# Attention and two expert layers on one core: token pairs become the outer loop, decoded weights pass through DRAM, partial outputs stay in SBUF

## The chip, the cores and the metric

The kernel runs on one core of one Trainium2 chip. The metric is the device time of one execution in microseconds (us). A measurement of this kernel tells a change of about 0.2% from no change. The engines that the text speaks of are PE (TensorE: matmuls, with PEld for its weight loads), DVE (VectorE), ACT (ScalarE), POOL (GpSimd) and SP (SyncE, which only issues DMAs here). Each works through its own queue of instructions in order; a DMA is issued by an instruction in the queue of SP or ACT and then runs by itself.

## The reference

The first stage is attention with a block-causal mask for 4 batches, 8 heads, 576 positions, 64 wide; its output, 2304 tokens by 512, is x of two feed-forward layers (512 to 2048 to 512):

```python
def _moe_ref(x, w_in, w_out, alpha):
    h = x @ w_in
    g = np.maximum(h, 0.0) + alpha * np.minimum(h, 0.0)
    return g @ w_out

def _moe2_ref(x, w_in, w_out):
    h = x @ w_in
    g = np.where(h > 0.0, h, np.exp(np.minimum(h, 0.0)) - 1.0)
    return g @ w_out

x = attn_out.transpose(0, 2, 1, 3).reshape(2304, 512)
x = _moe_ref(x, w_in, w_out, alpha)
return _moe2_ref(x, w2_in, w2_out)
```

The weights arrive as 64-bit floats.

## The kernel before, in words

Every operand of a matmul is split into a high and a low part (`act.copy` or a cast makes the high part, `low_part` subtracts it), and a product is three matmul passes, `PASSES`: high by high, high by low, low by high.

**Weights.** `load_word` fetches 128 rows of 512 64-bit words (512 KB) and rebuilds 32-bit floats: two activations on ACT (L135, L136), three operations on DVE (L140, L141, L145), one addition on POOL (L150). `load_in` decodes two such words and makes of them the seven Strassen variants of a pair of blocks of w_in: four sums or differences 256 wide (on POOL, L195 to L198), a cast on ACT, a low part on DVE. `load_out` decodes one word of w_out. Both leave their result in SBUF, where three blocks of work use it. There are 64 words in all.

**Attention** takes the first part of the program, with one quarter of layer 1 (4 of 16 blocks of the hidden width) for the tokens that are ready beside it. `plain_tail` is the rest of this quarter: products of the last two token units (512 and 256 tokens), before and among the first Strassen steps.

**The Strassen part** is the other three quarters of layer 1 (`layer == 0`) and all of layer 2 (`layer == 1`). The 2304 tokens are six chunks of N = 384, taken in pairs p = 0, 1, 2; the hidden width is taken in groups g of four blocks of 128. A block of work (layer, g, p) has two halves, each with seven products of six matmuls 384 wide (`product`, L702) in three PSUM banks, so 14 steps and 84 of these matmuls; the `outputs` of the block before (96 matmuls in layer 1, L795; 72 in layer 2, 512 wide, L797) run in between. `BLOCKS` lists 9 blocks of layer 1 and 12 of layer 2: g is the outer loop, p runs forth and back inside.

- `fetch` and `convert` make the seven variants of x for a pair: sums 768 wide (L657), a cast on ACT (L661) and a low part (L97) on DVE or POOL. They run for each change of (layer, p).
- `hiddens` copies a bank to SBUF after four of the seven products (`keep`, L739, on ACT), adds three of these on POOL (`add`, L744) and joins two more on DVE from a bank (L767, L772). One group of results is gated from its bank, three from SBUF, each 384 wide (`gated`): layer 1 has an activation (L715) and a DVE operation (L718); layer 2 an exponential on ACT (L721) and two DVE operations (L722, L723). Then come the cast (L724) and a low part (L97), half of them on POOL.
- `outputs` loads the partial sum z of each of its pieces from DRAM (`zd`, `yd`), adds the bank to it on DVE (L802) and stores it again.

All of these DMAs are issued by SP. In the Strassen part PE's order is that in which the code emits the work; the order on the other engines is laid by the scheduler.

## Time and profile before

| | |
|---|---|
| time, median of 3 runs (lowest to highest) | 1133.84 us (1132.81 to 1134.96) |
| the profiled execution's own time | 1132.23 us |
| its span, first to last instruction | 1130.4 us |
| PE busy, share of the span | 983.5 us, 87% |
| DVE busy | 891.9 us, 79% |
| POOL busy | 694.9 us, 61% |
| ACT busy | 585.4 us, 52% |
| bytes moved by DMA | 170.17 MB, mean 151 GB/s |

The span is 1.8 us shorter than the time of the same execution. Shares are averages over the attention part and the Strassen part, which have different limits, so the stretches have to be read apart. PE's clock is granted by a throttle, at 1.00 (2.4 GHz) or less.

### The profile page before, as it was taken

Reading aid. Unit: us, or ns where it says so; the run is one execution under the profiler, and the core shown is the slowest. Engines: PE = TensorE matmul, PEld = TensorE weight load, DVE = VectorE, ACT = ScalarE, POOL = GpSimd, SP = SyncE. Lnnn points to the kernel's source line nnn. Section 1 sums busy time; section 2 is a strip of 40 time slices with the busy share of each in tenths; the row PEclk is TensorE's granted clock in tenths of the full one; section 3 lists DMA queues with packets and bytes.
Section 4 is the critical chain, followed back from the end, with each engine's and each line's share of the span. In section 5 each row is a group of like instructions: output and inputs, shape, how many; then the busy total and the mean of one; then the engine's idle time right before and its main releaser. Section 6 shows DMA issues by size and latency. Waiting matters only on the chain.

```text
span 1130.4 us, 16131 instructions
## 1 busy us (share of the span) xinstructions
PE 983.5 (87%) x5300; PEld 852.3 (75%) x5300; DVE 891.9 (79%) x1386; ACT 585.4 (52%) x1305; POOL 694.9 (61%) x660
## 2 busy tenths in 40 slices
PE   4878999899984879797988978888988998899998
PEld 3556677567774779797978978877877887798886
DVE  5885576775799989697869798998799879967753
ACT  5875476565455345453545365554645454445431
POOL 5876576672677866457645675585658564835530
PEclk9889999999986899999998989999999999899999
DMA  5453323513775464747473745432354454434333
GB/s 179 146 176 124 95 88 101 192 48 106 241 265 177 163 215 150 236 139 229 152 235 126 222 129 174 131 112 84 117 156 156 140 157 143 137 106 145 107 103 121
DMA packets 101381, 170.17 MB, mean 151 GB/s; under 512 B 15792, under 2 KB 61360, under 8 KB 101296
## 3 DMA queue, kind: packets, MB, share of 16 engines
q1 hardware_dynamic: 101008, 168.87, 47.1%
q8 instruction: 42, 0.69, 0.2%
q14 instruction: 43, 0.35, 0.1%
q10 hardware_dynamic: 288, 0.26, 0.1%
HBM read 121.91 MB, written 47.19 MB: 150 GB/s over the span
## 4 chain that ended last, share of the span: by engine, by line
PE 31%; DVE 30%; DMA 12%; issue 10%; POOL 10%; ACT 5%; SPq 1%; POOLq 0%; ACTq 0%; DVEq 0%
PE bank L702 8%; PE bank L797 7%; DMA wraw<-w 6%; DVE xr L657 4%; PE bank L483 3%; DVE xv L97 3%; PE pair L338 3%; PE bank L601 2%; POOL wword L150 2%; DVE wword L140 2%; DVE g L97 2%; PE bank L612 2%; POOL snap L744 2%; DVE e L722 2%; DVE wword L145 2%
## 5 line engine op out<-in xcount | busy, mean ns | idle before, releaser
L702 PE MATMUL bank<-xv,wv 128*128 128x384 f32 x1764 | 380.6, 354 | 98.6 <-DVE snap L772 54.0
L702 PEld LDWEIGHTS bank<-xv,wv 128*128 128x128 f32 x1764 | 328.8, 199 | 128.5 <-DVE snap L772 64.5
L797 PE MATMUL bank<-wo,g 128*128 128x512 f32 x864 | 228.2, 399 | 2.6 <-ACT g L724 1.9
L744 POOL TENSOR_TENSOR snap<-snap 128x384 f32<-128x384 f32 x126 | 154.5, 1229 | 60.6 <-ACT snap L739 53.5
L797 PEld LDWEIGHTS bank<-wo,g 128*128 128x128 f32 x864 | 163.3, 192 | 28.1 <-ACT g L724 2.4
L795 PE MATMUL bank<-g,wo 128*128 128x384 f32 x864 | 181.0, 350 | 0.5 <-POOL g L97 0.5
L795 PEld LDWEIGHTS bank<-g,wo 128*128 128x128 f32 x864 | 162.0, 199 | 0.8 <-POOL g L97 0.8
L150 POOL TENSOR_TENSOR wword<-wword,wraw 128x512 int32<-128x512 int32 x64 | 95.6, 1495 | 63.7 <-DVE wword L145 47.7
L97 POOL TENSOR_TENSOR g<-e,g 128x384 fp32r<-128x384 f32 x48 | 62.7, 1307 | 95.5 <-ACT g L724 93.8
L104 POOL TENSOR_SCALAR p<-p,stat 128x128 f32<-128x128 f32 (+4 forms) x144 | 84.3, 601 | 49.7 <-DVE stat L397 32.9
L657 DVE TENSOR_TENSOR xr<-xr 128x768 f32<-128x768 f32 x71 | 88.9, 1253 | 27.3 <-POOL xr L657 11.7
L802 DVE TENSOR_TENSOR z<-bank,z 128x384 f32<-128x384 f32 (+1 forms) x126 | 76.3, 605 | 34.1 <-PE bank L797 27.4
L724 ACT CAST g<-e 128x384 fp32r<-128x384 f32 x96 | 48.7, 509 | 97.6 <-DVE e L723 97.6
L739 ACT COPY snap<-bank 128x384 f32<-128x384 f32 x168 | 78.8, 472 | 28.9 <-PE bank L702 27.9
L661 ACT CAST xv<-xr 128x768 fp32r<-128x768 f32 x91 | 75.6, 836 | 29.7 <-DVE xr L657 17.7
L388 ACT ACTIVATE p<-pair,stat 128x128 f32<-128x128 f32 (+4 forms) x144 | 78.1, 555 | 22.6 <-DVE stat L361 22.0
L97 DVE TENSOR_TENSOR xv<-xr,xv 128x768 fp32r<-128x768 f32 x57 | 78.8, 1385 | 13.9 <-ACT xv L661 13.9
L97 POOL TENSOR_TENSOR xv<-xr,xv 128x768 fp32r<-128x768 f32 x34 | 72.3, 2125 | 25.0 <-ACT xv L661 24.8
L97 POOL TENSOR_TENSOR g<-snap,g 128x384 fp32r<-128x384 f32 x36 | 43.7, 1216 | 65.0 <-ACT g L724 65.0
L722 DVE TENSOR_SCALAR e<-e 128x384 f32<-128x384 f32 x96 | 59.3, 620 | 17.6 <-ACT e L721 16.4
L361 DVE TENSOR_REDUCE stat<-pair 128x2 f32<-128x256 f32 (+3 forms) x80 | 63.2, 807 | 5.7 <-PE pair L344 4.1
L145 DVE SCALAR_TENSOR_TENSOR wword<-wraw,wword 128x512 uint32<-128x512 uint32 x64 | 66.3, 1039 | 1.2
(99 smaller groups left out, 1661.5 us busy)
## 6 DMA issues: line engine op xcount, KB each, us to landing
wraw<-w SPq DMA_DIRECT2D x64, 512.0 KB, 4.3
zd<-z SPq DMA_DIRECT2D x84, 192.0 KB, 2.6
xv<-xd SPq DMA_DIRECT2D x42, 384.0 KB, 5.1
z<-zd SPq DMA_DIRECT2D x72, 192.0 KB, 2.6
xr<-zd SPq DMA_DIRECT2D x36, 384.0 KB, 3.3
yd<-z SPq DMA_DIRECT2D x54, 256.0 KB, 2.0
z<-yd SPq DMA_DIRECT2D x54, 256.0 KB, 2.6
xr<-xd SPq DMA_DIRECT2D x28, 384.0 KB, 3.7
```

What stands on the lines that cost most here:

```text
L97: return {"v": dve, "p": pool_e}[eng].tensor_tensor(out=out, in0=x, in1=f32(high), op=ALU.subtract)
L104: return pool_e.tensor_scalar(out, x, 1.0 if scale is None else scale, 1.0, ALU.mult, ALU.mult)
L145: dve.scalar_tensor_tensor(out=wi, in0=high, scalar=0xC0000000, in1=wi, op0=ALU.bitwise_and, op1=ALU.bitwise_or)
L150: pool_e.tensor_tensor(out=w, in0=w, in1=units, op=ALU.add)
L388: act.activation(out=out, in_=x, func=AF.Exp, bias=stat[:, k:k + 1], accum_out=stat[:, SUMS + 2 * k:SUMS + 2 * k + 1])
L657: tt = lambda eng, out, a, b, op: eng.tensor_tensor(out=out, in0=a, in1=b, op=op)
L702: pe.matmul(bank_, w[:, wp_, IN.index(wname), kc * P:kc * P + P], x[:, xp_, kc, :], start=start and kc == 0 and t == 0, stop=stop and kc = ...
L722: dve.tensor_scalar(g, g, 1.0, -1.0, ALU.min, ALU.add)
L739: act.copy(s, x)
L744: pool_e.tensor_tensor(out=out, in0=x, in1=y, op=ALU.add)
L795: pe.matmul(acc, w_out(0, f, wp_, m * P, P), gs[f, h][:, gp_, :], start=s, stop=e)
L797: pe.matmul(acc, gs[f, h][:, gp_, m * P:m * P + P], w_out(1, f, wp_, 0, DM), start=s, stop=e)
```

## The change

- `BLOCKS`: the pair p is now the outer loop, g the inner one. x's variants are made once for each (layer, p): 6 times; the order before made them 16 times.
- z of a pair stays in SBUF (`zall`) over all its groups; it is stored once per layer and pair, and in layer 1 loaded once per pair.
- A decoded weight goes from a staging tile (one `wvs`, one `wos`) to DRAM (`wvd`, `wod`), and each half-block fetches its variants of w_in (1792 KB), each block its two parts of w_out (1024 KB each), from there. These fetches, those of x and those of z are issued by ACT; raw words and stores are issued by SP, whose order is now that of the code too. The sums of `load_in` move from POOL to DVE, and more words are decoded during attention (four `load_in` and four `load_out`; before two `load_in`).
- `hiddens` has another order of products: two banks accumulate on; three copies (two to c2, one to p1) and three joins on DVE from a bank (L763) replace four copies, three POOL additions and two DVE joins.
- `gated` works on two blocks at once, 768 wide: c2 as a whole, of c1 one half from SBUF and one from the bank. In layer 2 a second activation on ACT takes the place of DVE's L722. All its low parts are DVE's.

```diff
+    def load_out(layer, f):
+        t = stage_p.tile([P, 2, DM], F32R, tag="wo", name="wos")
...
+            def store():
+                j, i = divmod(f, 2)
+                if (layer, j) not in wod:
+                    wod[layer, j] = dram.tile([P, 2, 2, DM], F32, name=f"wod{layer}_{j}")
+                nc.sync.dma_start(out=wod[layer, j][:, i], in_=f32(t))
...
-            tt = pool_e.tensor_tensor
+            tt = SUMS_ON.tensor_tensor
...
+    SUMS_ON = dve
+    LAG_IN = 3
...
-    BLOCKS = [(0, g, p) for g, p in block_order(range(1, 4))] + [(1, g, p) for g, p in block_order(range(4))]
+    BLOCKS = [(0, g, p) for p in range(NC // 2) for g in range(1, 4)] + [
+        (1, g, p) for p in range(NC // 2) for g in range(4)]
...
+    def gated(layer, f0, c, last, low):
...
+        quarters = [c[:, 0], c[:, 1] if last is None else last]
+        e = e_p[0].tile([P, 2, N], F32, tag="e", name="e")
...
-            act.activation(out=g, in_=c, func=AF.Exp)
-            dve.tensor_scalar(g, g, 1.0, -1.0, ALU.min, ALU.add)
-            dve.scalar_tensor_tensor(out=g, in0=c, scalar=0.0, in1=g, op0=ALU.max, op1=ALU.add)
-        act.copy(t[:, 0], g)
-        low_part(low, t[:, 1], g, t[:, 0])
+            activate(e, c, AF.Exp)
+            act.activation(out=e, in_=e, func=AF.Relu, scale=-1.0, bias=1.0)
+            for out, x, y in ((c, c, e),) if last is None else [(c[:, i], x, e[:, i]) for i, x in enumerate(quarters)]:
+                dve.scalar_tensor_tensor(out=out, in0=x, scalar=0.0, in1=y, op0=ALU.max, op1=ALU.subtract)
+        act.copy(t[:, 0], c)
+        low_part(low, t[:, 1], c, t[:, 0])
...
+        def join(s, x, y):
             with tc.high_priority(offset=URGENT):
-                pool_e.tensor_tensor(out=out, in0=x, in1=y, op=ALU.add)
+                dve.tensor_tensor(out=s, in0=x, in1=y, op=ALU.add)
+        product(b, w, "11", v["11"], True, False)
+        keep(p1, b)
+        product(d, w, "s1", v["t1"], True, False)
+        keep(c2[:, 1], d)
+        product(b, w, "s2", v["t2"], False, False)
+        keep(c2[:, 0], b)
+        product(a, w, "12", v["21"], True, True)
+        join(c1[:, 0], a, p1)
+        product(b, w, "s3", v["t3"], False, False)
+        join(c2[:, 1], b, c2[:, 1])
+        product(d, w, "s4", v["22"], False, True)
+        join(c2[:, 0], d, c2[:, 0])
+        gs[j, 1] = gated(layer, f0, c2, None, "v")
+        product(b, w, "22", v["t4"], False, True)
+        gs[j, 0] = gated(layer, f0, c1, b, "v")
...
-        arrival[0] = 4
...
+        def fetch_in(half):
...
+            wv[half] = w = wv_p.tile([P, 2, 7, HD], F32R, tag="wv", name="wv")
+            nc.scalar.dma_start(out=f32(w), in_=wvd[layer, j])
...
+        for half in range(2 * N_BLOCKS):
+            at(HALFB * (half - 1) + 1 if half > 1 else 2 * half - LEAD_IN, lambda half=half: fetch_in(half))
```

(The lines of `hiddens` are drawn together: allocations and `yield`s are left out.) With `arrival[0]` left at 2, a raw word is now asked for two steps ahead of its first activation in the Strassen part; before it was four.

How the order moves on PE, in a half-block of layer 2. Before (L702 are the products of one half in banks 3111 to 3113, L797 the outputs of the block before):

```order
L702 MATMUL bank_3111<-xv,wv 128x384 x6
L797 MATMUL bank_3115<-wo,g_8697 128x512 x3
L797 MATMUL bank_3115<-wo,g_8786 128x512 x3
L702 MATMUL bank_3112<-xv,wv 128x384 x6
L797 MATMUL bank_3116<-wo,g_8526 128x512 x3
L797 MATMUL bank_3116<-wo,g_8616 128x512 x3
L702 MATMUL bank_3111<-xv,wv 128x384 x6
L797 MATMUL bank_3116<-wo,g_8697 128x512 x3
L702 MATMUL bank_3113<-xv,wv 128x384 x6
```

And now (L717 are the products, L819 the outputs):

```order
L717 MATMUL bank_3226<-xv,wv 128x384 x6
L819 MATMUL bank_3229<-wo,g_7798 128x512 x6
L717 MATMUL bank_3227<-xv,wv 128x384 x6
L819 MATMUL bank_3230<-wo,g_7688 128x512 x6
L717 MATMUL bank_3226<-xv,wv 128x384 x6
L819 MATMUL bank_3230<-wo,g_7798 128x512 x3
L717 MATMUL bank_3228<-xv,wv 128x384 x6
L819 MATMUL bank_3230<-wo,g_7798 128x512 x3
L819 MATMUL bank_3231<-wo,g_7688 128x512 x3
```

The count of matmuls is the same; a bank comes back two steps after its last product, in three places of a half, and the bank that is gated last is written again as `a` in step 3 of the half that follows.

On DVE, in a late block of layer 2 where no weight is decoded. Before (`snap` are copies of banks, `e` the gating):

```order
L722 TENSOR_SCALAR e<-e 128x384
L767 TENSOR_TENSOR snap<-bank_3112,snap 128x384
L723 SCALAR_TENSOR_TENSOR e<-snap,e 128x384
L97 TENSOR_TENSOR xv<-xr,xv 128x768
L722 TENSOR_SCALAR e<-e 128x384
L772 TENSOR_TENSOR snap<-bank_3111,snap 128x384
L723 SCALAR_TENSOR_TENSOR e<-snap,e 128x384
L97 TENSOR_TENSOR xv<-xr,xv 128x768
L657 TENSOR_TENSOR xr<-xr 128x768
```

And now, one half with its three joins (`c` holds c1 or c2, `p` the copy p1):

```order
L763 TENSOR_TENSOR c_8353<-bank_3228,p_8311 128x384 [waits PE_49]
L763 TENSOR_TENSOR c_8328<-bank_3226,c_8328 128x384 [waits PE_49]
L826 TENSOR_TENSOR zall<-bank_3231,zall 128x512 [waits PE_49]
L763 TENSOR_TENSOR c_8328<-bank_3227,c_8328 128x384 [waits PE_49]
L744 SCALAR_TENSOR_TENSOR c_8328<-c_8328,e 128x768 [waits DVE_49,Activation_49]
L98 TENSOR_TENSOR g_8382<-c_8328,g_8382 128x768 [waits Activation_49]
L826 TENSOR_TENSOR zall<-bank_3232,zall 128x512 [waits PE_49]
L744 SCALAR_TENSOR_TENSOR c_8353<-c_8353,e 128x384 [waits Activation_49]
L744 SCALAR_TENSOR_TENSOR c_8353<-bank_3226,e 128x384
L98 TENSOR_TENSOR g_8402<-c_8353,g_8402 128x768 [waits Activation_49]
```

The x operations and L722 are gone from this stretch, the joins are three, and the additions to z wait for PE alone.

On ACT, in a block of layer 2 while weights are being decoded, now (L951 fetches w_in, L958 w_out; L136 and L137 begin a raw word; L188 makes the high part in the staging tile):

```order
L951 DMA wv<-wvd_7_6693 128x3584 [waits DMAHW0_49,PE_49]
L188 CAST wos<-wword 128x512 [waits DMAHW0_49,Pool_49]
L745 CAST g_7098<-c_7042 128x768 [waits DVE_49]
L734 ACTIVATE e<-c_7069 128x384 [waits Activation_49]
L734 ACTIVATE e<-bank_3228 128x384
L759 COPY p_7137<-bank_3226 128x384 [waits PE_49]
L136 ACTIVATE wword<-wraw 128x512 [waits DMAHW1_49]
L137 ACTIVATE wraw<-wraw 128x512
L742 ACTIVATE e<-e 128x768 [waits Activation_49]
L759 COPY c_7154<-bank_3227 128x384 [waits PE_49]
L958 DMA wo<-wod_6_6760 128x2048 [waits DMAHW4_49,PE_49]
```

Before, ACT's queue held no DMA in this part; now fetches, and waits for DMAs that have to land (DMAHW), stand in the queue that copies banks for PE.

## Rows read from the trace of the kernel before

**Rows 1.** Windows of the Strassen part, one per block: length, busy per engine, clock, DMA.
```profile
313.00:345.50 32.50, 23.86 (x135) 22.08 (x133) 30.86 (x35) 17.00 (x39) 26.49 (x21) 0.89 0.69 247
...
517.10:553.70 36.60, 33.55 (x182) 32.99 (x181) 27.79 (x39) 16.04 (x32) 24.49 (x22) 0.95 0.57 196
...
632.30:670.50 38.20, 34.75 (x182) 34.12 (x182) 31.75 (x39) 20.09 (x38) 24.13 (x17) 0.91 0.47 147
670.50:712.10 41.60, 35.48 (x182) 34.51 (x182) 38.47 (x50) 22.37 (x42) 28.68 (x21) 0.92 0.52 165
...
787.70:821.10 33.40, 31.57 (x158) 27.92 (x157) 24.01 (x36) 21.47 (x43) 20.56 (x17) 1.00 0.38 116
...
1010.10:1041.20 31.10, 31.10 (x158) 28.22 (x157) 19.18 (x30) 14.61 (x27) 16.57 (x13) 1.00 0.38 123
...
1073.70:1105.50 31.80, 31.09 (x155) 27.65 (x154) 18.54 (x35) 12.62 (x27) 11.27 (x11) 1.00 0.34 101
1105.50:1130.40 24.90, 20.98 (x90) 16.57 (x89) 7.36 (x12) 1.41 (x3) 1.71 (x2) 1.00 0.39 127
```

**Rows 2.** Waits in 313 to 1105 us: engine, line, releaser, total us, times, longest.
```profile
PE bank L702 <- DVE snap L772: 54.0, 24, 5.4
...
PE bank L702 <- ACT snap L739: 26.4, 15, 5.3
...
ACT wword L135 <- DMA wraw<-w: 22.6, 14, 5.0
ACT wraw L136 <- DMA wraw<-w: 17.8, 14, 2.4
```

**Rows 3.** A window with the clock at 1.00 in layer 1, and the attention part.
```profile
540.00:560.00 20.00, 19.93 (x114) 19.38 (x113) 17.50 (x26) 10.52 (x22) 12.61 (x12) 1.00 0.46 150
0.00:280.00 280.00, 240.00 (x1593) 171.27 (x1594) 185.29 (x454) 174.58 (x505) 180.69 (x282) 0.96 0.41 126
```

**Rows 4.** Single lines and their instructions: ns minimum, median, maximum; first and last start.
```profile
L657 DVE TENSOR_TENSOR xr<-xr x71: 941/954/2067, 299.0 to 1069.4; 128x768 f32<-128x768 f32 x71
L140 DVE TENSOR_SCALAR wword<-wword x64: 407/439/1669, 14.3 to 961.4; 128x512 f32<-128x512 f32 x64
L145 DVE SCALAR_TENSOR_TENSOR wword<-wraw,wword x64: 673/693/2359, 15.3 to 962.8; 128x512 uint32<-128x512 uint32 x64
...
L263 ACTq DMA_DIRECT2D qraw<-qT x2: 404/432/460, 0.7 to 1.2; - x2
```

**Rows 5.** Groups by line and shape: busy us, mean ns, idle before and its releaser.
```profile
L722 DVE TENSOR_SCALAR e<-e 128x384 f32<-128x384 f32 x96 | 59.3, 620 | 17.6 <-ACT e L721 16.4
L802 DVE TENSOR_TENSOR z<-bank,z 128x384 f32<-128x384 f32 x72 | 39.3, 546 | 2.6 <-PE bank L795 2.5
L802 DVE TENSOR_TENSOR z<-bank,z 128x512 f32<-128x512 f32 x54 | 36.9, 684 | 31.5 <-PE bank L797 27.4 <-DMA z<-yd 4.1
L772 DVE TENSOR_TENSOR snap<-bank,snap 128x384 f32<-128x384 f32 x42 | 23.0, 549 | 0.8 <-PE bank L702 0.8
L723 DVE SCALAR_TENSOR_TENSOR e<-bank,e 128x384 f32<-128x384 f32 x24 | 13.3, 556 | 0.7
L718 DVE SCALAR_TENSOR_TENSOR gf<-neg,beta,bank 128x384 f32<-128x384 f32 x18 | 10.9, 603 | 2.2 <-ACT neg L715 2.2
L661 ACT CAST xv<-xr 128x768 fp32r<-128x768 f32 x91 | 75.6, 836 | 29.7 <-DVE xr L657 17.7 <-issue 5.5 <-DMA xr<-zd 4.4
```

**Rows 6.** POOL's two costliest groups in the Strassen part, same columns.
```profile
L744 POOL TENSOR_TENSOR snap<-snap 128x384 f32<-128x384 f32 x126 | 154.5, 1229 | 60.6 <-ACT snap L739 53.5 <-PE bank L797 4.2 <-PE bank L795 2.7
L150 POOL TENSOR_TENSOR wword<-wword,wraw 128x512 int32<-128x512 int32 x64 | 95.6, 1495 | 63.7 <-DVE wword L145 47.7 <-issue 8.5 <-DMA zd<-z 2.0
```

**Rows 7.** Two windows with much DMA, columns as in Rows 1.
```profile
314.00:319.00 5.00, 0.26 (x2) 0.00 (x0) 4.97 (x5) 1.35 (x4) 3.53 (x3) 0.90 1.03 403
310.00:330.00 20.00, 14.37 (x85) 13.44 (x84) 18.55 (x21) 10.00 (x21) 14.77 (x11) 0.83 0.90 323
```

**Rows 8.** The page's DMA issues: size of one, median us to landing.
```profile
wraw<-w SPq DMA_DIRECT2D x64, 512.0 KB, 4.3
```

More of the change, by code (lines that the diff above doesn't have):

```diff
@@ L738, in keep, with hiddens @@
+    def hiddens(layer, j, w, v, gs):
+        a_, b_, d_ = banks = rings["p"]
+        rings["p"] = [b_, a_, d_]
+        a, b, d = (bank[i][:, :N] for i in banks)
+        f0 = 2 * j
+        def keep(s, x):
             with tc.high_priority(offset=URGENT):
                 act.copy(s, x)
-            return s
-        def add(out, x, y):
+        def join(s, x, y):
             with tc.high_priority(offset=URGENT):
-                pool_e.tensor_tensor(out=out, in0=x, in1=y, op=ALU.add)
-        product(a, w, "11", v["11"], True, False)
@@ L773, in hiddens, with z_part @@
-        gs[f1, 0] = gated(layer, f1, p1, "p", p1)
+        gs[j, 0] = gated(layer, f0, c1, b, "v")
         yield
-    def z_tile():
-        return z_p[0].tile([P, DM], F32, tag="z", name="z")
-    def outputs(layer, g, p, gs, order):
-        for h in range(2):
-            c = 2 * p + h
-            for m in range(KC if layer == 0 else N // P):
-                n = N if layer == 0 else DM
-                acc = bank[take("z")][:, :n]
-                where = zd[c][:, m, :] if layer == 0 else yd[c][:, m, :]
-                z = z_tile()[:, :n]
-                begun = layer == 0 or g > 0
-                if begun:
-                    nc.sync.dma_start(out=z, in_=where)
-                for i, f in enumerate(order):
+    def z_part(layer, h, m):
+        n, per = (N, KC) if layer == 0 else (DM, N // P)
+        return zall[0][:, n * (per * h + m):n * (per * h + m) + n]
@@ new lines, in outputs, with store @@
+    def outputs(layer, g, p, gs):
+        last = g == 3
+        def store(h, m, z):
+            c = 2 * p + h
+            if layer == 0:
+                nc.sync.dma_start(out=zd[c][:, m, :], in_=z)
+                if p < NC // 2 - 1:
+                    later(2, lambda: load_z(p + 1, h, m))
+            else:
+                for r, part in rows(c, m):
+                    nc.sync.dma_start(out=out[r:r + part.stop - part.start, :], in_=z[part, :])
+        for h in (1, 0):
+            for m in range(KC if layer == 0 else N // P):
+                acc = bank[take("z")][:, :N if layer == 0 else DM]
+                z = z_part(layer, h, m)
+                for i in range(4):
+                    j, k = 2 * g + i // 2, i % 2
@@ L802, in outputs @@
                         dve.tensor_tensor(out=z, in0=acc, in1=z, op=ALU.add)
-                else:
-                    copy("av"[m % 2], z, acc)
-                if layer == 1 and g == 3:
-                    for r, part in rows(c, m):
-                        nc.sync.dma_start(out=out[r:r + part.stop - part.start, :], in_=z[part, :])
-                else:
-                    nc.sync.dma_start(out=where, in_=z)
+                if last:
+                    later(1, lambda h=h, m=m, z=z: store(h, m, z))
@@ L892, in attention_moe_kernel @@
                 k = to
[L893 to L896 removed]
+        assert not held and not halves and not jobs
+    with tc.manual_schedule(engines={ET.PE, ET.SP}):
         att.close()
@@ L995, in attention_moe_kernel @@
                 done += 1
+        while due:
+            end_tick()
+        assert not work
 def kernel(q, k, v, moe_w_in, moe_w_out, moe_alpha, moe2_w_in, moe2_w_out):
```

281 lines of the change are left out of this document (140 added, 141 removed).

## The prediction

> **What bounds the kernel now.** I read the page's shares first: PE 87%, DVE 79%, no engine full, so the stretches decide. The second view, the busy time in one window per block [rows 1], cuts the span in five: 313.0 us up to the first Strassen matmul; 357.5 for the nine blocks of layer 1 (313.0 to 670.5); 117.2 for the first three of layer 2 (to 787.7); 317.8 for the last nine (to 1105.5); 24.9 for the outputs of the last block alone. The reader is to see two things there. PE has a floor: in layer 1 a window with the clock at 1.00 holds 114 matmuls in 19.93 us [rows 3], 0.175 each, and a block has 84 + 96 = 180: 31.5 us. In layer 2 the last outputs run 90 in 20.98 us, 0.233 each, and 84 x 0.175 + 72 x 0.233 is 31.5 again. And the length of a block follows DVE: with 18.5 or 19.2 us of DVE work it takes 31.8 and 31.1, with 24.0 it takes 33.4, with 27.8 36.6, with 31.8 38.2, with 38.5 41.6. The third view, the waits, says why: PE stood 54.0 us for the DVE join L772 and 26.4 for ACT's copy L739 [rows 2]; where it stood, its clock was granted at 0.91 to 0.95. So a change is worth what it does to DVE's work per block, as long as its own waits stay short.
>
> **The change, part by part.** I cost DVE by operations that nothing disturbed. The x sum takes 0.941 at least and 0.954 in the median, and 2.07 at most [rows 4]: the long ones lie beside POOL's operations. So 768 wide is 0.95; 384 wide from a bank 0.55 or, with beta, 0.60; an addition to z 0.55 or 0.68 [rows 5]; the three decoding operations 0.43 + 0.43 + 0.69 = 1.55 a word [rows 4].
>
> *x variants.* 16 conversions become 6. The order counts 36 sums on DVE and POOL where 92 stood, 33 low parts for 91, 33 casts for 91. Off ACT go 58 x 0.836 = 48 us [rows 5].
>
> *Products and gating.* Joins on DVE go from 4 to 6 a block (+1.1 us), the POOL additions, 154.5 us in all, vanish [rows 6]; so do the 96 L722, 59.3 us of DVE [rows 5], for 48 ACT operations 768 wide, for which the nearest row is the cast, 0.84: 40 us. No row has DVE gating 768 wide; the x sum, of the same width and also from SBUF, bounds it from below with 0.95, two of 384 from above with 1.10; I take 0.95, since its shape is the nearer. A block of layer 2 then has joins 6 x 0.55 = 3.3, z 6 x 0.68 = 4.1, gating and low parts 4 x 0.55 + 6 x 0.95 = 7.9, together 15.3 us of DVE. A block of layer 1 has 3.3, z 8 x 0.55 = 4.4, gating 8 x 0.60 = 4.8 and low parts 4 x 0.95 = 3.8, together 16.3. These operations are on the path only through DVE's total, since joins come first in its queue.
>
> *Decoding.* By the order's steps 35 of the 64 words fall in the nine layer 1 blocks, 7 in the next three, none in the last nine, where the trace has them up to 963 us [rows 4]. 35 x 1.55 = 54, and the sums (now DVE's, four of about 0.42 a pair), high and low parts add some 30.
>
> *Sums for DVE.* Layer 1: 9 x 16.3 = 147, 32 x operations at 0.95 = 30, decoding 84: 261 us, 29.0 a block. What POOL still does there (L150 and a few x operations, about 52 instructions in the first twelve blocks) can cost DVE nothing or up to 2.07 - 0.94 = 1.1 us each [rows 4], 57 us; I take a third, 19, or 1.6 a block. That makes 30.6. Between 27.8 (36.6 us long) and 31.8 (38.2 long) this is worth about 36.5 a block: 9 x 36.5 = 328. Next three: 74 us in the count, 24.7 + 1.6 = 26.3 a block, between 24.0 (33.4) and 27.8 (36.6): 34.7, so 104. Last nine: 149 us, 16.5 a block; seven without a conversion sit on the floor like the rows with 18.5 and 19.2 (31.8 with the slower), two with one carry about 22 and get 33.3: 289.
>
> *The port.* The long DVE operations of rows 4 lose 1.1 us at most beside a POOL operation. The Trainium skill, "SBUF — State Buffer", section "Who interferes with whom", says that a DVE operation with two SBUF inputs and a GpSimd operation that reads SBUF exclude each other for a whole instruction; by it each of the 52 could hold DVE for its own 1.5 us, 78 us where I count 19, and the time would be some 40 us later. The median of 0.954 beside a maximum of 2.07 shows that most do not meet, so the row decides.
>
> *Attention.* Eight more words and four sets of sums come in: 8 x 1.55 + 12.5 for parts and sums = about 26 us of DVE. DVE is busy 185 of the first 280 us, PE 240 [rows 3]. Fully hidden it costs 0, fully exposed 26; I take 8. Weights for the first block must now be fetched, but eight hidden products of the tail (48 x 0.233 + 48 x about 0.13 = 17 us) cover the 4.2 MB that it needs first, 10.4 us at 403 GB/s [rows 7]. I leave the start at 313 + 8; if the cover fails, up to 10 more.
>
> *DMA.* By tile sizes z takes 47 MB less and x 24 less, but weights are fetched, 42 x (1.84 + 1.05) = 121 MB, and stored, 40: 170 becomes about 260. By the code's steps the second to eleventh block move 12.1, 14.7, 13.4, 8.9, 15.5, 12.6, 9.2, 13.2, 11.3 and 10.8 MB. A fetch of w_in has seven steps of 31.5 / 14 = 2.25 us to land, 15.8 us for 1.84 MB, which take 4.6 at 403 GB/s [rows 7]. At this rate the two heaviest blocks need 36.5 and 38.5 us; both carry a conversion, so DVE makes them longer than the mean of 36.5 anyway, and I add nothing. The Trainium skill, "DMA: Bandwidth & Descriptors", section "Specifications", gives 358 GB/s as the HBM limit of a core; by that these two take 41 and 43 us, some 9 us more in the sum. The window with 403 GB/s is over it, so I keep the row.
>
> *ACT's queue.* 144 issues at 0.43 [rows 4] are 62 us, against 48 of casts that leave and 40 of second activations that come: ACT stays near half busy (17 to 22 us in blocks of 31 to 42 [rows 1]), and its idle time hides the issues. Each is placed behind the product that frees its buffer; behind it in the queue stand the cast and the gating of the same half and the next copy of a bank. Without that cover the issues cost up to their 62.
>
> *Sum.* 313 + 8 + 328 + 104 + 289 + 25 = 1067 of span, + 1.8 to the profiled execution's time, 1069, which stands 1.6 us under the median of the runs: 1070 us, against 1133.84.
>
> **The rivals.**
> *DMA becomes the bound* in the blocks up to the eleventh. For it: the best 20 us window holds 323 GB/s [rows 7]. At that rate the blocks with 13 MB and more take 41, 45, 41 and 48 us where DVE gives about 38: 7 + 3 + 10 + 3, with some 5 for their neighbours +28, 1098 us. Against it: small pieces fill that window, weight rows are long.
> *The gating chain becomes PE's wait in layer 2.* The bank gated last must be free by step 3 of the next half, four steps or 9.0 us after the join of c2. One tile `e` serves both: exponential 0.84, second activation 0.84, DVE 0.95, exponentials 1.0, activation 0.84, two DVE operations 1.1, with the join 6.1 us, plus queues. If it is 1.5 us late in each of 24 halves: +36, 1106 us. Today the chain holds snapshots, not banks, in three groups of four.
> *PE sits on its floor everywhere.* 313 + 4 + 21 x 31.8 + 27 = 1012 us. For it: the last blocks do. Against it: DVE at 29 us a block while words are decoded.
> *ACT's queue holds PE up: slower.* A raw word is now asked for two steps ahead instead of four, 4.5 us, and its landing is 4.3 in the median [rows 8] before any of the new traffic; ACT waits for raw words 40 us already [rows 2]. A wait there stands in front of the copies that PE needs one step later. At 2.4 us of PE per word for 42 words it is +101, 1171; from 64 / 42 = 1.5 us per word on the change is a loss.
> *The freed DVE time buys nothing*, because PE waits as often for six joins as for four: about 1132.
>
> **How the numbers follow.** The forecast has 0.58 (its own range 1040 to 1090), DMA 0.12, the chain 0.10, the floor 0.05, ACT's queue 0.11, nothing 0.04. 0.2%, about what a measurement here tells from no change, is 2.3 us. Faster: 0.58 + 0.12 + 0.10 + 0.05 = 0.85; slower 0.12, the queue and a bit of the last; same 0.03. The range leaves out the floor, the queue and the last: 1035 to 1118.
>
> **What the profile after would show.** Right: the last nine blocks at 31 to 33 us, clock 1.00, DVE under 23 in each; DVE near 30 in the first nine and no PE wait on a join over some 15 us in total; POOL under 300 us; the x sums near 0.95 in the mean as well. Wrong: a DMA share above 0.9 over whole blocks with PE waiting for `wv` (the first rival), PE waiting on L744's last gating (the second), ACT idle for `wraw` or a store over 100 us with PE on L759 (the fourth), or the first Strassen matmul later than 335 us.

## The result and the profile after

The changed kernel takes 1082.25 us in the median (1080.92 to 1084.74, four runs), the kernel before, timed beside it, 1133.55: a ratio of 0.9549, 95% interval 0.9528 to 0.9569. The forecast was 1070, in a range of 1035 to 1118. The profiled execution's span is 1080.9 us against 1130.4.

I number the 21 blocks 0 to 20; a block's window runs from its first product to the next block's. By stretches, against the terms of the prediction's sum:

| us | before | predicted | after |
|---|---|---|---|
| start, to the first Strassen product | 313.0 | 321 | 337.1 |
| blocks 0 to 8 (layer 1) | 357.5 | 328 | 332.2 |
| blocks 9 to 11 | 117.2 | 104 | 105.5 |
| blocks 12 to 20 | 317.8 | 289 | 281.7 |
| last outputs | 24.9 | 25 | 24.5 |

The first row does not compare equal work. Before the change, 48 of the output products of the tail ran ahead of the first Strassen product; now they run in block 0, which has 180 matmuls where it had 135 [rows 1]. The stretch up to the first Strassen product, before and after, and these 48 products before:

```profile
0.00:313.00 313.00, 271.64 (x1760) 196.64 (x1761) 210.25 (x486) 190.93 (x534) 201.37 (x297) 0.96 0.44 137
...
0.00:337.10 337.10, 266.94 (x1713) 191.16 (x1713) 240.22 (x533) 203.38 (x558) 210.90 (x297) 0.94 0.56 185
...
300.70 11.07 PE L831 MATMUL bank<-gs,w 128*128 128x512 f32 x48
```

On equal work, by an estimate that moves these 11.1 us, the start is 35 us later and blocks 0 to 8 are 36 us shorter.

First the page: busy time of each engine, what DMA moved, the queue of ACT, and the DMA issues (KB each, median us to landing).

```profile
PE 964.7 (89%) x5300; PEld 840.6 (78%) x5300; DVE 723.6 (67%) x1293; ACT 544.0 (50%) x1127; POOL 293.8 (27%) x351
...
DMA packets 80346, 260.38 MB, mean 241 GB/s; under 512 B 13328, under 2 KB 45584, under 8 KB 67728
...
q10 hardware_dynamic: 21312, 143.79, 35.7%
...
wv<-wvd ACTq DMA_DIRECT2D x42, 1792.0 KB, 8.1
wo<-wod ACTq DMA_DIRECT2D x42, 1024.0 KB, 7.9
wraw<-w SPq DMA_DIRECT2D x64, 512.0 KB, 7.7
```

DVE lost 168 us of work, POOL 401, PE 19 (its mean clock is 0.956, before 0.947). DMA moved 260 MB where it had moved 170, and a raw word, of unchanged size, lands in 7.7 us where it took 4.3 [rows 8]. Then the windows, one per block, columns as in [rows 1]: blocks 0 to 6, 8 to 10, 14, the attention part, and last the stretch from 280 us to the end of block 8.

```profile
337.10:370.60 33.50, 33.29 (x180) 30.75 (x181) 26.27 (x43) 17.11 (x33) 8.01 (x6) 0.95 0.59 203
370.60:421.30 50.70, 35.39 (x164) 33.77 (x163) 30.68 (x51) 18.64 (x32) 6.98 (x5) 0.76 0.84 338
421.30:453.00 31.70, 31.70 (x182) 31.51 (x181) 26.27 (x44) 16.84 (x29) 7.87 (x5) 1.00 0.86 312
453.00:494.50 41.50, 33.95 (x182) 33.00 (x181) 32.83 (x56) 16.79 (x29) 6.68 (x5) 0.92 0.84 341
494.50:528.20 33.70, 31.90 (x182) 31.58 (x181) 22.26 (x40) 14.54 (x26) 4.44 (x3) 1.00 0.98 369
528.20:559.70 31.50, 31.50 (x182) 31.50 (x181) 26.98 (x47) 17.63 (x31) 6.22 (x4) 1.00 0.90 327
559.70:593.50 33.80, 32.15 (x182) 31.50 (x181) 29.91 (x48) 14.93 (x25) 2.76 (x2) 1.00 0.92 372
...
629.20:669.20 40.00, 33.38 (x182) 32.73 (x181) 35.46 (x59) 19.23 (x33) 9.25 (x5) 0.91 0.87 324
669.20:700.80 31.60, 31.60 (x182) 31.60 (x181) 27.55 (x41) 18.68 (x31) 6.46 (x4) 1.00 0.83 310
700.80:740.30 39.50, 35.11 (x161) 31.26 (x160) 25.39 (x45) 19.27 (x34) 5.30 (x4) 0.87 0.78 289
...
837.70:869.00 31.30, 31.30 (x158) 28.18 (x157) 13.06 (x20) 14.24 (x23) 0.00 (x0) 1.00 0.55 202
...
0.00:280.00 280.00, 229.20 (x1521) 163.01 (x1522) 209.19 (x485) 183.91 (x520) 190.02 (x283) 0.96 0.48 153
...
280.00:669.20 389.20, 334.32 (x1794) 317.48 (x1793) 283.85 (x469) 171.62 (x300) 78.78 (x53) 0.92 0.87 327
```

The reader is to see three things. Blocks with 26.3, 27.0 and 27.6 us of DVE work run 31.7, 31.5 and 31.6, on PE's floor; before, 27.8 went with 36.6 [rows 1]. The long blocks (50.7, 41.5, 40.0, 39.5) have a DMA share of 0.78 to 0.87, and their clock is at 0.76 to 0.92. In the first 280 us DVE has 24 us more work than before and PE has done 11 less [rows 3].

What PE waited for from 337.1 us on (columns as in [rows 2]):

```profile
PE bank L817 <- DMA wo<-wod: 15.7, 3, 7.6
PE bank L717 <- DVE c L738: 8.8, 5, 3.1
PE bank L717 <- ACT p L759: 6.4, 4, 2.4
PE bank L817 <- DVE zall L826: 5.9, 1, 5.9
PE bank L717 <- DVE c L744: 4.6, 4, 2.4
...
PE bank L717 <- DVE c L763: 0.9, 2, 0.7
```

The join that had cost 54.0 us [rows 2] costs 0.9. The largest wait is new: the fetch of w_out. Last, two places of the timeline (start, length, instruction, in brackets the idle time before it and what ended it): ACT and PE at the end of attention, and PE in block 1.

```profile
299.63 4.68 ACTq L661 DMA_DIRECT2D xr<-xd  x4
306.81 0.60 ACTq L684 DMA_DIRECT2D xv<-xd  x1
307.46 0.66 ACT L136 ACTIVATE wword<-wraw 128x512 f32<-128x512 f32 x1 [14.15 <-DMA zd<-z]
...
308.58 0.36 ACT L506 CAST x<-bank 128x256 fp32r<-128x256 f32 x1
...
308.99 0.79 PE L844 MATMUL bank<-x,w 128*128 128x512 f32 x1 [10.69 <-ACT x L506]
...
386.19 2.29 PE L817 MATMUL bank<-g,wo 128*128 128x384 f32 x6 [7.64 <-DMA wo<-wod]
```

ACT computes nothing for 14.15 us: in its queue stand five fetches of x for the first block, the fifth issued at 306.8, and behind them the casts of attention's last output, for which PE waits 10.69 us. The end of the idle time is put down to a store of z that landed.

### The profile page after: what moved, and what is told of

The parts are those of the page before. It is cut to its first block, busy times and chain, and to the rows that moved or that the text cites. A ratio compares the mean times of both kernels' runs of the same rounds, so it can differ in the third digit from the quotient of the medians.

```text
span 1080.9 us, 14875 instructions
## 1 busy us (share of the span) xinstructions
PE 964.7 (89%) x5300; PEld 840.6 (78%) x5300; DVE 723.6 (67%) x1293; ACT 544.0 (50%) x1127; POOL 293.8 (27%) x351
## 2 busy tenths in 40 slices
DMA packets 80346, 260.38 MB, mean 241 GB/s; under 512 B 13328, under 2 KB 45584, under 8 KB 67728
## 3 DMA queue, kind: packets, MB, share of 16 engines
q1 hardware_dynamic: 58960, 115.63, 30.6%
## 4 chain that ended last, share of the span: by engine, by line
PE 54%; DVE 16%; DMA 16%; ACT 5%; issue 4%; POOL 3%; SPq 1%; ACTq 0%; POOLq 0%; DVEq 0%
PE bank L717 21%; PE bank L819 16%; PE bank L817 8%; DMA wraw<-w 7%; DMA xv<-xd 2%; PE bank L618 2%; PE bank L500 2%; DVE wword L146 2%; DVE stat L378 2%; DMA xr<-xd 2%; PE pair L355 2%; PE bank L629 1%; DVE wword L141 1%; ACT p L405 1%; DMA wod<-wos 1%
## 5 line engine op out<-in xcount | busy, mean ns | idle before, releaser
L717 PE MATMUL bank<-xv,wv 128*128 128x384 f32 x1764 | 365.5, 343 | 23.4 <-DVE c L738 8.8
L717 PEld LDWEIGHTS bank<-xv,wv 128*128 128x128 f32 x1764 | 320.8, 192 | 43.7 <-DVE c L738 10.4
L819 PE MATMUL bank<-wo,g 128*128 128x512 f32 x864 | 225.9, 396 | 0.0
L819 PEld LDWEIGHTS bank<-wo,g 128*128 128x128 f32 x864 | 161.2, 189 | 24.6
L731 ACT ACTIVATE e<-c 128x768 f32<-128x768 f32 x42 | 35.5, 846 | 158.5 <-DVE c L763 152.0
L98 DVE TENSOR_TENSOR g<-c,g 128x768 fp32r<-128x768 f32 x84 | 82.4, 981 | 40.0 <-ACT g L745 39.8
L745 ACT CAST g<-c 128x768 fp32r<-128x768 f32 x84 | 70.2, 835 | 67.3 <-DVE c L738 34.6
L826 DVE TENSOR_TENSOR zall<-bank,zall 128x384 f32<-128x384 f32 (+1 forms) x126 | 76.5, 610 | 32.5 <-PE bank L819 27.4
L763 DVE TENSOR_TENSOR c<-bank,c 128x384 f32<-128x384 f32 x84 | 46.6, 555 | 56.1 <-PE bank L717 55.8
L744 DVE SCALAR_TENSOR_TENSOR c<-c,e 128x768 f32<-128x768 f32 (+1 forms) x48 | 38.8, 809 | 46.5 <-ACT e L742 46.5
L98 POOL TENSOR_TENSOR xv<-xr,xv 128x768 fp32r<-128x768 f32 x9 | 19.1, 2117 | 178.0 <-DVE c L744 113.8
L136 ACT ACTIVATE wword<-wraw 128x512 f32<-128x512 f32 x64 | 43.1, 673 | 48.3 <-DMA wraw<-w 25.6
L500 PE MATMUL bank<-pt,vraw 128*64 128x320 f32 (+3 forms) x448 | 56.5, 387 | 0.6 <-DVE x L98 0.5
L759 ACT COPY c<-bank 128x384 f32<-128x384 f32 x84 | 39.8, 479 | 29.2 <-PE bank L717 28.7
L500 PEld LDWEIGHTS bank<-pt,vraw 128*64 128x64 f32 (+1 forms) x448 | 29.4, 143 | 29.3 <-issue 12.0
```

The source lines that it names most:

```text
L98: return {"v": dve, "p": pool_e}[eng].tensor_tensor(out=out, in0=x, in1=f32(high), op=ALU.subtract)
L500: pe.matmul(op[64 * x:64 * x + 64, lo:qn], s["v"][:rows, x, j, :], s["pt"][:rows, x, o + lo:o + qn], start=j == 0, stop=j == chunks[-1], s ...
L717: pe.matmul(bank_, w[:, wp_, IN.index(wname), kc * P:kc * P + P], x[:, xp_, kc, :], start=start and kc == 0 and t == 0, stop=stop and kc = ...
L745: act.copy(t[:, 0], c)
L763: dve.tensor_tensor(out=s, in0=x, in1=y, op=ALU.add)
L819: pe.matmul(acc, x[:, m * P:m * P + P], w[:, wp_, :], start=s, stop=e)
```

## The experiments

All in one table first: median, ratio to the kernel before with its interval (of single runs the time alone), and the stretches of the profiled execution, which can lie some us from the median (e6 1080.87, e11 1078.90, e14 1061.51).

| run | us | ratio, 95% | start | 0–8 | end of 8 | 9–11 | 12–20 |
|---|---|---|---|---|---|---|---|
| after | 1082.25 | 0.9528–0.9569 | 337.1 | 332.2 | 669 | 105.5 | 281.7 |
| e1_start_on_sp | 1073.24 | 0.9456–0.9521 | 314.5 | 347.0 | 661 | 103.9 | 281.5 |
| e2_wo_in_w0 | 1080.37 | 0.9517–0.956 | 332.5 | 334.0 | 666 | 104.4 | 281.4 |
| e3_sums_on_pool | 1081.08 | 0.9498–0.9562 | 337.5 | 332.2 | 670 | 103.6 | 283.5 |
| e4_copies | 1149.96 | one run | 338.0 | 360.7 | 699 | 112.5 | 312.4 |
| e5_four_words_less | 1071.0 | one run | 325.2 | 333.9 | 659 | 104.1 | 281.6 |
| e6_arrival4 | 1077.24 | 0.9457–0.9535 | 338.4 | 325.6 | 664 | 105.3 | 285.4 |
| e7_low_on_pool | 1087.62 | 0.9568–0.9624 | 337.9 | 338.0 | 676 | 103.5 | 282.1 |
| e8_convert_always | 1089.51 | one run | 335.4 | 333.9 | 669 | 104.6 | 289.4 |
| e10_sp_and_lead | 1066.69 | 0.9373–0.9456 | 317.1 | 344.6 | 662 | 96.3 | 283.2 |
| e11_all_on_sp | 1081.85 | 0.9505–0.9575 | 313.1 | 355.3 | 668 | 98.2 | 285.8 |
| e12_three | 1070.46 | 0.9409–0.9471 | 316.8 | 344.9 | 662 | 95.6 | 285.4 |
| e14_high_of_wo | 1057.26 | 0.9283–0.9346 | 337.7 | 314.2 | 652 | 102.1 | 281.4 |

My theory after the result: joins and DVE no longer hold PE; the start lost 16 us more than foreseen by ACT's hold and by decoding beside attention; the long blocks up to 10 wait for DMA. The rivals: DVE's work still sets the length of a block, or single transfers and buffers are badly placed and the load of the DMA engines does not matter.

### The start

**e1_start_on_sp.** SP issues the first block's fetches:

```diff
-                nc.scalar.dma_start(out=t, in_=xd[hi][:, k, kc:kc + 2, :])
+                q.dma_start(out=t, in_=xd[hi][:, k, kc:kc + 2, :])
...
+            (nc.scalar if half > 1 else nc.sync).dma_start(out=f32(w), in_=wvd[layer, j])
```

> The fetches for the first block (its two halves of w_in, x for the first pair) are issued by SP; all later ones stay with ACT. Theory: the changed kernel starts its first Strassen matmul at 337.1 us, 24.1 later than before, and about 11 of these come from ACT's queue, which stood still for 14.2 us (293.3 to 307.5) at DMA issues ahead of the last casts of attention. Then the start moves to 323 to 328 and the time to about 1071 (1068 to 1075). Rival: the DMA engines themselves are full there (379 GB/s from 300 to 320 us), the casts were late for another reason and x arrives no sooner; then the start stays at 334 or later and the time within 3 us of 1082.

The first Strassen product came 22.6 us earlier, at 314.5, which is more than the 323 to 328 expected. So the hold of ACT's queue was real and dearer than the 10.69 us of PE's one wait: from the tail's first product to the first Strassen product it takes 41.1 us in after, at a granted clock of 0.79, and 20.8 us here, at 1.00. But blocks 0 to 8 became 14.8 longer, block 0 alone 11.2 (33.6 to 44.8). The end of block 8 moved by 8.

**e5_four_words_less.** Four words of w_out are not decoded beside attention; zeros are stored in their place.

> The decoding of the four words of w_out beside attention is left out (zeros are stored in their place, so the stores stay). Theory: attention ended 12.8 us later than before (first product of the tail at 296.0 against 283.2) because of the 26 us of DVE work and 17 of ACT that came in; four words are about 9 us of that DVE work, so the tail starts 3 to 6 us earlier and the time is 1076 to 1080. Rival: the words lie in idle time and the stores and fetches are what is late; then the tail starts at 295 or later and nothing moves.

The tail's first product came at 284.5 us, with them at 296.0 (before the change at 283.2). The other runs that decode these words have it between 292.2 and 297.5, so 8 to 13 us, most of the 12.8 by which attention became longer, are the price of these four words. It need not be DVE's share of it, as the next run shows. The gain is more than the 3 to 6 us expected, and the time lies 5 us below the theory's range. Here everything behind the start came earlier with it: x for block 0 was asked for at 288.6 (in after at 299.6), blocks 0 to 2 kept their lengths (33.8, 50.6 and 31.8 us), and of the 11.9 us won at the start 10 were left at the end of block 8.

**e3_sums_on_pool.** `SUMS_ON = pool_e` in place of `dve`.

> The sums of load_in go back to POOL, as in the kernel before; nothing else changes. DVE loses some 27 us in all, of which 6 to 7 beside attention (four sets of four). Theory that DVE's work beside attention lies exposed: the tail's first product comes 4 to 8 us earlier; the first nine blocks gain at most 3 us, since they wait for PE or DMA. Time 1072 to 1079. By the length that follows DVE, the first nine blocks gain 12 us more: 1062 to 1067. If POOL's longer sums (about twice DVE's time) hold the staging tile, and with it the store and the next word, the time is no better than 1082.

The tail's first product did not come earlier (296.0), nor did the layer 1 blocks shorten: a miss for both expectations that named a gain. DVE's busy time fell by 10 us where 27 were expected, POOL's rose by 51. So it makes no difference to the time which of the two engines does the sums, and which of a word's operations (ACT two, DVE three, POOL one, casts, a low part) lies exposed beside attention stays open.

### What sets the length of a block

**e8_convert_always.** The last nine blocks make x's variants anew each time (`b > 11 or` in the condition).

> In the last nine blocks x is fetched and its variants made anew for every block, not once per pair: seven conversions more, each 9 DVE operations of 0.95 us and 2 MB. Theory now: a block stays on PE's floor (31.3 us) as long as DVE has under about 28 us, as the blocks with 26.3, 27.0 and 27.6 us of DVE did (31.7, 31.5, 31.6); with 14 + 8 = 22 us nothing happens, the time is 1080 to 1086. Rival, the step of the prediction: the length of a block follows DVE as before, 24 us make 33.4; then the last nine blocks grow by 1.5 to 2 us each and the time is 1093 to 1098.

The time, 1089.51 in one execution, lies between the two ranges: a miss for both. The last nine blocks took 289.4 us against 281.7. Of these 7.7 us 5.7 fall in block 12 (37.0 us with 27.6 of DVE work), where ACT waited 4.6 us until a fetch of x had landed and PE 3.6 for the gating in L744. The others ran 30.8 to 32.4 with 16 to 24 us of DVE work. So more DVE work costs almost nothing in these eight; that the late fetch made block 12 long fits the trace, but no run shows it. In the changed kernel these conversions are thus worth some 8 of the 36 us by which the nine blocks became shorter.

**e7_low_on_pool.**

```diff
-        gs[j, 0] = gated(layer, f0, c1, b, "v")
+        gs[j, 0] = gated(layer, f0, c1, b, "p")
```

> The low parts of c1 go from DVE to POOL, as half of the gated low parts were on POOL in the kernel before. DVE loses two operations of 0.95 us a block, 40 us in all. If the length of a block followed DVE's work as the prediction had it (3.8 us of DVE between 33.4 and 36.6 us of length), the first twelve blocks become 1.6 us shorter each, 19 us in all, time 1063. Theory that blocks below 28 us of DVE lie on PE's floor and the longer ones wait for DMA: the first twelve lose at most 5 us, and the later gating (POOL takes 2.0 us for a 768 wide low part, DVE 0.98) or the port can give a few back: time 1076 to 1088.

It was 5 us slower, not 19 faster. But this run says nothing on what the first nine blocks wait for, since there DVE's busy time did not fall (252.8 us in after, 253.2 here). Most of the fall is in the last nine, from 145.3 to 130.6, and their length stayed (281.7 and 282.1). The page of this run:

```profile
PE 966.6 (89%) x5300; PEld 841.5 (77%) x5300; DVE 705.7 (65%) x1251; ACT 544.6 (50%) x1127; POOL 375.6 (35%) x393
```

42 operations of 0.98 us left DVE, 41 us, but its busy time fell by 17.9 only (723.6 to 705.7). The other 23 us came back on DVE, 0.55 for each operation that POOL took over, most of it as longer DVE operations: added up, they lie some 20 us further above the shortest of their kind than in after.

**e4_copies.** Two copies of 1 MB in each block, DRAM to DRAM, issued by SP:

```diff
+            extra = dram.tile([P, 4 * DM], U32, name=f"extra{b}_{i}")
+            nc.sync.dma_start(out=extra, in_=(w1, w2)[layer][b % 8].bitcast(U32))
```

> SP additionally issues two DRAM to DRAM copies of 1 MB in every block (44 MB in all that nothing reads), placed where the w_out halves are fetched. Theory that the DMA engines are near their limit in blocks 1 to 10: these moved 9.8 to 17.1 MB each at 312 to 372 GB/s; with 2.1 MB more at 372 GB/s the blocks 1 to 11 together become 20 us longer by transport alone, and up to 55 us where landings come later in a row; the last nine, at 185 to 256 GB/s, stay at 31 to 32 us each. Time 1100 to 1140. Rival, that single landings placed badly (not the engines' load) made the long blocks: every block within 1 us of what it was, time below 1090.

Slower by 68 us, 10 beyond the theory's range. The blocks 0 to 11 gave 36 of it, within what was expected; the other 31 fell in the last nine, where I had expected none: 1.6 us for each of some 18.9 MB, in blocks whose DMA share in after was 0.36 to 0.71. So a MB has its price also where the DMA engines are far from full on the average. (The rates of blocks 1 to 10 in after begin at 289 GB/s, in block 10, not at 312.) The windows of its blocks 13 and 14, and of 280 us to the end of block 8 (for the next run):

```profile
844.60:890.00 45.40, 34.85 (x157) 30.49 (x157) 19.88 (x28) 14.58 (x23) 1.81 (x1) 0.85 0.85 316
890.00:927.70 37.70, 31.53 (x158) 27.89 (x156) 16.45 (x24) 17.24 (x28) 0.00 (x0) 0.98 0.94 355
...
280.00:698.60 418.60, 335.74 (x1797) 318.41 (x1796) 285.51 (x473) 171.78 (x302) 79.60 (x53) 0.91 0.91 344
```

One place of the timeline in block 13, on ACT and on PE:

```profile
859.77 0.83 ACT L676 CAST xv<-xr 128x768 fp32r<-128x768 f32 x1 [10.33 <-DMA xr<-zd]
...
862.71 0.47 ACT L759 COPY c<-bank 128x384 f32<-128x384 f32 x1
...
863.23 2.29 PE L717 MATMUL bank<-xv,wv 128*128 128x384 f32 x6 [9.37 <-ACT c L759]
```

A fetch of x lands late, the cast that needs it stands first in ACT's queue, the copy of a bank stands behind the cast, and PE waits 9.37 us for that copy. This is the way by which a late transfer reaches PE though PE itself waits for no transfer.

**e14_high_of_wo.** Half of each fetch of w_out; the products use the high part twice:

```diff
-                            pe.matmul(acc, w[:, wp_, m * P:m * P + P], x, start=s, stop=e)
+                            pe.matmul(acc, w[:, 0, m * P:m * P + P], x, start=s, stop=e)
...
-            nc.scalar.dma_start(out=f32(w), in_=wod[layer, j])
+            nc.scalar.dma_start(out=f32(w[:, :, 0]), in_=wod[layer, j][:, :, 0])
```

> Only the high part of w_out is fetched, 512 KB a piece in place of 1024, 22 MB less in all; the output's products use the high part where they used the low one, as many matmuls as before. Theory that transport holds the long blocks of 1 to 11: with 1.05 MB less a block, 2.8 us at 372 GB/s, these lose 12 to 30 us together, most where PE waits for w_out (block 1, 50.7 us, below 46); the last nine stay; time 1053 to 1071. Rival, that the long blocks come from the place of single DMAs and buffers in the queues, whatever their size: the wait for w_out moves by the 2 to 4 us that one landing becomes shorter, and the time is 1075 to 1084.

25 us faster, within the theory's range and outside the rival's. Blocks 0 to 8 lost 18.0 us, the last nine nothing (281.4). Block 1 fell to 45.1, block 8 from 40.0 to 31.9, without a change in the order of anything. This is its window from 280 us to the end of block 8, to be read beside the last rows of the windows of after and of e4_copies:

```profile
280.00:651.90 371.90, 330.93 (x1797) 315.26 (x1797) 283.72 (x467) 169.84 (x299) 79.55 (x52) 0.94 0.85 314
```

Length by rate gives 116.8 MB here, 127.3 in after and 144.0 in e4_copies. With 10.5 MB less the stretch is 17.3 us shorter, with 16.7 MB more 29.4 longer: 1.65 and 1.76 us a MB in both directions, where a MB at the 372 GB/s of block 6 takes 2.7. About two thirds of the transport shows in the time. (A MB of a copy is both read from and written to DRAM, so the two prices are not of quite the same thing.) The same three rows have DVE busy for 283.7, 283.9 and 285.5 us: the length moves by 47 us while DVE's work stays. So layer 1 gets longer and shorter with the bytes at equal DVE work; and in e3, with 6.8 us less of DVE work in blocks 0 to 8 (246.0), they took 332.2 us as in after.

### Moving single waits

**e2_wo_in_w0.** Two allocations change places, so that the first w_out tile lies where the plain weights lay and can be fetched sooner.

> Only the order of two allocations changes, so that the tiles of w_out lie where the plain weights lay and no longer where the tail keeps z. Theory: the second block took 50.7 us because its first fetch of w_out was issued at 374.0, after the last z store of the tail had landed, and PE stood 9.9 us for it at a clock of 0.76; with the new place the fetch waits for PE's last product of the tail alone, the block takes 38 to 42 and the time is 1071 to 1075. Rival: the fetch is slow because the queue of ACT and the DMA engines are full with z, w_in and raw words; then PE still waits over 6 us there and the time stays above 1079.

Block 1 fell from 50.7 to 38.1, and block 3 rose from 41.5 to 59.7. There, in the timeline of ACT and of PE:

```profile
472.06 0.92 ACT L217 CAST wvs<-wword 128x512 fp32r<-128x512 f32 x2 [11.81 <-DMA wvd<-wvs]
...
461.63 1.33 PE L817 MATMUL bank<-g,wo 128*128 128x384 f32 x3 [11.22 <-DMA wo<-wod]
480.11 2.29 PE L717 MATMUL bank<-xv,wv 128*128 128x384 f32 x6 [11.14 <-DVE c L763]
```

The wait moved: to the next fetch, and to ACT's cast into the one staging tile, whose store had not landed. Block 1 did what the theory said, the time (1080.37, its interval overlaps that of after) what the rival said.

**e6_arrival4.** `arrival[0] = 4` at the start of the Strassen part, as before the change.

> In the Strassen part a raw word is asked for four steps ahead of its first activation in place of two, as in the kernel before; the decoding itself falls two steps later. Theory that ACT, held for raw words that land in 7.7 us (it waited 23.5 us for them between 337 and 780 us), passes this on to PE by its late copies and to DVE by late words: ACT's waits for wraw fall below 5 us, and the first twelve blocks lose 3 to 10 us, time 1072 to 1079. Rival, that ACT's stay is hidden by its idle half and the DMA engines set the length there: within 3 us, 1079 to 1085.

5 us faster in the median, inside the theory's range; the interval overlaps that of after, and the profiled execution is the slowest of the four. ACT's waits for raw words fell less than expected (to 10.2 us in L136). Layer 1 gained 6.6, the last nine blocks lost 3.7. PE's wait for w_out is no longer among its long ones, but its wait for a join rose from 0.9 to 11.2 us: here too a wait moved.

**e10_sp_and_lead, e12_three, e11_all_on_sp.** The first two join edits above; in the third every `nc.scalar.dma_start` is `nc.sync.dma_start`.

> The edits of two runs together: the first block's fetches issued by SP (1073.24 alone) and raw words asked for four steps ahead (1077.24 alone), against 1082.25 without either. Theory that each removes a hold of ACT's queue of its own: the gains add, 9 + 5, time 1066 to 1070. Rival, that the DMA engines set the pace of blocks 0 to 10 (129 MB there, 348 us at 372 GB/s): what the start gains is given back, time 1072 to 1078.

> Three edits together: the first block's fetches issued by SP, the tiles of w_out in the space of the plain weights (so that the first of them can be fetched before the tail's z is stored), raw words asked for four steps ahead. Theory that block 1's wait for w_out and block 3's wait of ACT for the staging store are single late landings: with a longer lead block 3 gives less back, block 1 falls from 50 to below 40 us, time 1058 to 1068. Rival, that 348 us of transport in blocks 0 to 10 come out as a wait in one block or another: time 1070 to 1080.

> All fetches (x, z, w_in, w_out) are issued by SP in place of ACT, 144 issues; the same bytes in the same order of the code. Theory that ACT's queue is the place where a late landing or a buffer that is not free yet is passed on to PE's copies and to the decoding: the start comes some 20 us earlier as with the first block's fetches alone, and blocks 0 to 10 do not give it all back; time 1060 to 1073. Rival, that SP, in order too, then holds raw words and stores behind fetches that wait for PE: words are decoded later, blocks 1 to 10 become longer, time 1080 to 1110.

The gains of e1 and e6 add in the total, though not in their places (against e1, e10 gains 2.4 us in layer 1, where e6 had its gain, and 7.6 in blocks 9 to 11): 1066.69 us, the fastest version that computes all of it, 1.4% under the changed kernel; its interval lies wholly below that one's. The third edit on top took nothing off (1070.46, the rival's range): block 1 fell to 41.2, blocks 2 and 3 rose to 41.9 and 50.1. With all fetches on SP the start is the earliest of all, 313.1, and layer 1 the longest of these, 355.3; PE's wait for w_out doubles. SP stands at stores of words that are not decoded yet, for no more time than in after (143.9 and 160.8 us), but now with fetches queued behind them (PE's and SP's waits, and last SP's in after):

```profile
PE bank L817 <- DMA wo<-wod: 34.2, 8, 9.3
...
SPq L186 <- DVE wos L98: 143.9, 19, 18.8
...
SPq L186 <- DVE wos L98: 160.8, 18, 17.4
```

Read down the column "end of 8": the start varies by 24 us between e11 and after, the end of block 8 by 1. In all runs with the bytes of after up to there it lies between 661 and 676; the two that change what layer 1 moves leave this range, to 652 and 699. The exception is e5, at 659: it has 2 MB less before the start, and its fetches began 11 us earlier too. Moving an issue from ACT to SP did not bring that.

## Why the prediction was right, and where not

*The join and DVE's relief: right.* Conversions, additions and L722 left as counted, and most prices per operation held: a join 0.55, an addition to z 0.55 and 0.69, the 768 wide low part 0.98 (taken 0.95), the 768 wide gating 0.99 (between the bounds of 0.95 and 1.10). Layer 1's gating was dearer, 0.71 (taken 0.60), and so was the third decoding operation, 0.77 (taken 0.69):

```profile
L98 DVE TENSOR_TENSOR g<-c,g 128x768 fp32r<-128x768 f32 x84 | 82.4, 981 | 40.0 <-ACT g L745 39.8
L763 DVE TENSOR_TENSOR c<-bank,c 128x384 f32<-128x384 f32 x84 | 46.6, 555 | 56.1 <-PE bank L717 55.8
...
L738 DVE SCALAR_TENSOR_TENSOR c<-e,beta,c 128x384 f32<-128x384 f32 x54 | 36.7, 706 | 10.8 <-ACT e L731 10.7
L146 DVE SCALAR_TENSOR_TENSOR wword<-wraw,wword 128x512 uint32<-128x512 uint32 x42 | 32.5, 773 | 0.9
...
L744 DVE SCALAR_TENSOR_TENSOR c<-c,e 128x768 f32<-128x768 f32 x24 | 23.9, 994 | 39.1 <-ACT e L742 39.1
```

DVE is busy for 145.3 us in blocks 12 to 20 (149 predicted), 76.0 in 9 to 11 (79), 252.8 in 0 to 8 (275). My sums added up single operations; in the trace neighbouring operations overlap, and busy time counts the overlap once. Added up as I did, the three stretches hold 150, 82 and 277 us: the work was forecast well, but it should not have been set beside the busy times of [rows 1]. PE's wait for a join went from 54.0 us to 0.9. Of the 49.5 us by which the span fell, layer 2 gave 47.8 (117.2 + 317.8 to 105.5 + 281.7) and layer 1 25.3; the start took 24.1 back (36 and 35 on equal work). The rival of the gating chain stayed small: PE waited 8.8 us for L738 and 4.6 for L744.

*"The length of a block follows DVE": the step that failed.* The rows of before that I picked show both rise together, and I read one as the cause of the other. A row that I left out did not fit even then: 26.8 us of DVE work with a length of 32.5, where 27.8 had 36.6.

```profile
1041.20:1073.70 32.50, 31.62 (x158) 28.13 (x157) 26.84 (x39) 16.28 (x31) 17.83 (x13) 1.00 0.39 124
```

Now blocks 2, 5 and 9, with 26 to 28 us of DVE work, run at the floor. That DVE's work no longer prices a block is shown for the last nine by e8 (block 12 apart), for layer 1 by e14 and e4, with equal DVE work and lengths 47 us apart. So the last nine were predicted 7.3 us too long.

*Layer 1: nearly the right number for the wrong reason.* 328 came from 30.6 us of DVE work a block; 332.2 was measured, with 28.1. What moves its length is the bytes, the first rival's mechanism. Its price there was +28 on the whole; e14 and e4 show 1.7 us per MB. Of the 49 us by which layer 1 exceeds nine blocks of 31.5, e14 takes away 18; what holds the rest is not shown. I foresaw 260 MB rightly (260.38), but counted a block as covered when its bytes fit into its length at the best rate. They do not come evenly: block 1 alone had 17.1 MB (50.7 us at 338 GB/s), where I had put the heaviest at the third and the sixth. Of the sign that I gave for this rival, the DMA share above 0.9 showed (blocks 4 and 6), PE waiting for `wv` did not; the wait came by w_out, and by way of ACT's queue.

The Trainium skill, "DMA: Bandwidth & Descriptors", section "Specifications", gives 358 GB/s as a core's HBM limit. Block 6 moved 372 GB/s over 33.8 us, block 4 369 over 33.7: the trace does not stop there.

*The start: mis-sized.* Taken +8, measured +24.1, so that the first Strassen product came at 337.1, past the 335 that I had named as a sign of error: the tail began 12.8 us later (decoding of more words, e5), and from there to the first Strassen product it took 11.3 longer (41.1 against 29.8). The second part is larger on equal work: the 48 output products, 11 us, that stood in it before now run in block 0, so the eight hidden products alone took 22 us longer (41.1; with e1's edit 20.8). I kept 313 as the base though these products were no longer in it, so on equal work the term was 27 us too small, not 16. I had said "up to 10 more if the cover fails"; this was for a cause that I had not named: I took ACT's issues as hidden because ACT is half idle. Idle on the average does not help an instruction that stands behind a DMA issue (e1).

*ACT's queue as a rival:* its mechanism is real (e4, e6), at a small price. Waits for raw words (16.3 us in L136 and 7.2 in L137 between 337 and 780) reach PE only in part.

*The port: sized about right, from a misread row.* The 1.1 us that I gave as the most that one operation loses are not the most in [rows 4]: L145 took 2.359 at most and 0.673 at least, 1.7 us apart, with a POOL operation of 1.85 us beside it. After the change 49 POOL operations start in blocks 0 to 11 (52 counted), and the 91 DVE operations that overlap one last 22 us longer in all than the median of their kind; the others last no longer. That is near the 19 us that I took, and far from the 78 that the prediction worked out as a bound by the Trainium skill, "SBUF — State Buffer", section "Who interferes with whom". The x sums, 1.04 us in the mean where I named 0.95, lost 2 of the 22. Where POOL has 42 more operations (e7), 0.55 us is lost for each.

In sums: start +16.1, layer 1 +4.2, next three +1.5, last nine -7.3, last outputs -0.5 make the 14 us by which the span (1080.9) is over the predicted 1067. That the total came within some 12 us is in part luck: the last nine, predicted too long by a wrong rule, took back nearly half of what the start cost.

Left open: which engine makes a word beside attention dear; whether a second staging tile would help (not tried); and which part of the change freed PE in layer 2. No run takes back the new order of joins, the wider gating or the z kept in SBUF one at a time; e8 shows only that in the changed kernel the saved conversions are the smaller share.

## What to carry to other kernels

A relation between a block's length and an engine's work, read from the rows of before, is a cause only while that engine's waits hold PE; once they are gone, read the floor and look at what else fills the stretch. A loop order that saves conversions by moving weights through DRAM has to be priced in bytes per block against the rate the chip held over a whole block, and a removed wait can reappear at the next fetch: of 20 to 24 us won at the start by another issuing engine (e1, e10, e11, e12) 1 to 8 were left at the end of layer 1, while of the 11.9 us won where the fetches moved along (e5) 10 were left. A DMA issue or a cast that waits for a landing, placed in the queue of an engine that also copies banks for PE, turns that landing into PE's wait, however idle that engine is on the average.
